# Folding the adaLN modulation into the query and key weights, with a reordered front part, in an attention and MLP kernel on one core

## The chip, the core and the metric

The kernel runs on one core of one Trainium2 chip. A core has a matrix engine (PE, with its weight loads listed apart as PEld), a vector engine (DVE), a scalar engine (ACT), a general engine (POOL) and a sequencer that issues most transfers (SP). Each engine takes its instructions in the order in which the program lists them, and engines wait for each other by semaphores. The metric is the device time of one execution in microseconds (us).

## The reference

One transformer block on 2048 rows of 512 numbers, with 32 heads of 16 and one key and value head for all (MQA). `c` gives six modulation vectors; only the first two (`sa`, `ca`) matter to the change.

```python
mod = (_silu(c) @ w_mod).reshape(c.shape[0], 6, 1, -1)
sa, ca, ga, sb, cb, gb = ...
h = _layernorm(x, axis=-1) * (1 + ca) + sa
q = h @ wq ; k = h @ wk ; v = h @ wv
o = softmax(q k^T * 16**-0.5) v @ wo
x = x + ga * o
h = _layernorm(x, axis=-1) * (1 + cb) + sb
x = x + gb * (gelu(h @ w1 + b1) @ w2 + b2)
```

## The kernel before

Products that must be exact run as three: each operand is split into a high part (rounded to the fast format fp32r) and the remainder, and `mm3` (L165) adds high x high, low x high and high x low. So a projection of 512 columns over four slices of 128 is 12 matrix instructions.

The program has a front part and a main loop. The main loop takes 64 units (a unit is 256 rows by 4 pairs of heads); per step it computes scores (`sexp`, L617), their exponentials on ACT (L621), the products with the values (`pv`, L638), and beside them the row maxima of a later unit: `Max.step` issues one score product (L512) that DVE reduces (L517). The maxima run ahead of the loop, which starts when 56 of them are done. A unit has 32; the 48th of the front is the last one of unit 0. When a unit has its 32, `put_max` turns them (L565, L566), POOL splits them in high and low (L560, L133, L140), and four small transfers (L555) put them as rows 48 and 49 into the unit's query tile `qst`. For unit 0 two of the four are issued by ACT. The first score product of the main loop (`e`) waits for these four.

The front part, for four blocks of 512 rows: load x (L229), mean and variance on DVE (`stats1`, L206 to L212), a power on POOL (L214), normalise in place (`xhat1`: L373 on DVE or POOL, L371 on ACT), turn on PE (`turn1`, L380, into banks e0, e1, e2 in turn), modulate and split (`mod1`: ACT reads the turned bank with scale `ca1` and bias `sa` at L386, then L135, L133 and L140 split it into `hH` and `hL`), key and value products (`kv_products`), their copies out (`kv_out`, L401 and L402; `low_k` on DVE, L407; `repeat_k` on ACT, L411), the query projection of group g (`qproj`) with its weights split by `prep_wq` (L342, L343). Queries go to memory (`send_q`, L424) and come back in another layout by six transfers a unit (`load_q`, L483).

The modulation vectors come first: `mod_rows` (L297) multiplies with `w_mod`, `mod_cols` (L301) turns the result into columns.

All five instruction streams are recorded in program order. After block 0 that order is written out by hand: `SLOTS` is a list of steps, a number meaning so many maxima and a name one step of the named job (`heads b` is `turn1` and the split of one slice, `keys b` one slice of the key products, `wq g` a `prep_wq`, `rows` a slice of the remaining modulation vectors). `keep_warm` issues products whose results nobody reads (L292).

## Time and profile before

| | us |
|---|---|
| median of 3 runs | 1556.17 (1555.15 to 1556.21) |
| the profiled execution | 1555.99 |
| its span, first to last instruction | 1554.1 |
| PE busy | 1537.9 (99% of the span) |
| DVE busy | 1398.3 (90%) |
| ACT busy | 1230.4 (79%) |
| POOL busy | 683.7 (44%) |
| first reduction of a maximum starts | 33.17 |
| last maximum of unit 0 reduced | 69.53 |
| first score product of the main loop starts | 75.14 |

Times in views are us from the span's start. A row of the timeline or of the groups reads: line of the kernel, engine, operation, what it writes and what it reads, shapes, count; in brackets the idle time before and what ended it. Busy spans of PE overlap, since products are pipelined, so the step from one product to the next is read from their starts.

### The profile page before, as it was taken

What the parts mean: (1) busy time and instruction counts of PE and PEld (TensorE: products, weight loads), DVE (VectorE), ACT (ScalarE), POOL (GpSimd) and SP (SyncE); (2) the same over time, 40 slices, a digit from 0 to 9 for tenths busy, and PEclk for the clock granted to TensorE, in tenths of its full rate; (3) what the DMA queues carried; (4) which work ended last, traced back from release to release, by engine and by line L of the source; (5) the groups of instructions that cost most, each with busy time, mean ns of one, the idle gap of its engine ahead of it and who ended that gap; (6) DMA issues with size and microseconds to landing.
All of it is one profiled execution on the core that took longest, in us unless ns stands there. A gap on an engine that the chain in (4) does not pass through costs nothing.

```text
span 1554.1 us, 41556 instructions
## 1 busy us (share of the span) xinstructions
PE 1537.9 (99%) x16405; PEld 954.4 (61%) x16405; DVE 1398.3 (90%) x2488; ACT 1230.4 (79%) x2401; POOL 683.7 (44%) x1206
## 2 busy tenths in 40 slices
PE   7999999999999999999999999999999999999999
PEld 4455555567655665557655676556655676566658
DVE  7999999999999999999999999999999999999814
ACT  5577778788877887788877888788877888778874
POOL 5535432867422571246521563235711574046511
PEclk9999999999999999999999999999999999999999
DMA  7226412413030220303112120302212230203141
GB/s 240 102 89 199 151 57 81 130 51 97 18 105 26 72 68 28 103 19 109 33 51 79 56 87 16 111 26 88 68 30 73 60 101 25 87 28 99 48 150 48
DMA packets 84215, 120.85 MB, mean 78 GB/s; under 512 B 21342, under 2 KB 57438, under 8 KB 83764
## 3 DMA queue, kind: packets, MB, share of 16 engines
q1 hardware_dynamic: 84004, 118.18, 23.7%
q8 instruction: 130, 2.13, 0.6%
q14 instruction: 65, 0.53, 0.1%
q10 hardware_dynamic: 16, 0.00, 0.0%
HBM read 90.87 MB, written 26.74 MB: 76 GB/s over the span
## 4 chain that ended last, share of the span: by engine, by line
PE 86%; DVE 8%; issue 3%; POOL 2%; DMA 1%; ACT 0%; SPq 0%; POOLq 0%; DVEq 0%
PE acc L638 29%; PE m L512 23%; PE e L617 16%; PE w1ps L198 8%; DVE mx L517 6%; PE w2ps L198 2%; PE w2ps L188 2%; DMA xt<-in_A_x_dram 1%; PE w1ps L188 1%; PE wops L198 1%; PE tp L198 1%; PE qps L198 1%; PE kps L165 1%; DVE st L823 0%; DVE x L816 0%
## 5 line engine op out<-in xcount | busy, mean ns | idle before, releaser
L517 DVE TENSOR_REDUCE mx<-m 128x1 f32<-128x512 f32 x2048 | 1270.6, 682 | 86.6 <-PE m L512 65.1
L621 ACT ACTIVATE p<-e 128x512 f32<-128x512 f32 x2048 | 1098.8, 598 | 255.1 <-PE e L617 112.0
L512 PE MATMUL m<-ks,qst 64*128 64x512 f32 x2048 | 836.7, 429 | 2.0 <-DVE mx L517 0.6
L617 PE MATMUL e<-qst,ks 64*128 64x512 f32 x2048 | 740.2, 412 | 0.0
L638 PE MATMUL acc<-p,va 128*32 128x256 f32 x8192 | 548.0, 385 | 0.0
L512 PEld LDWEIGHTS m<-ks,qst 64*128 64x128 f32 x2048 | 368.2, 184 | 205.1 <-DVE mx L517 173.5
L617 PEld LDWEIGHTS e<-qst,ks 64*128 64x128 f32 x2048 | 359.6, 184 | 89.3 <-ACT p L621 62.5
L638 PEld LDWEIGHTS acc<-p,va 128*32 128x32 f32 x8192 | 214.0, 109 | 213.9 <-issue 110.9
L198 PE MATMUL w1ps<-h2H,w1t 64*128 64x256 f32 x1232 | 235.5, 287 | 0.0
L560 POOL TENSOR_SCALAR mt<-turned 8x32 f32<-8x32 f32 x256 | 53.1, 208 | 399.9 <-DVE turned L566 387.9
L198 PEld LDWEIGHTS w1ps<-h2H,w1t 64*128 64x128 f32 x1232 | 186.0, 185 | 28.9 <-DVE mx L517 14.8
L198 PE MATMUL w1ps<-h2L,w1t 64*128 64x256 f32 x616 | 169.3, 275 | 0.0
L198 PE MATMUL w2ps<-w2H,gH 64*128 64x512 f32 x274 | 120.3, 439 | 0.0
L198 PEld LDWEIGHTS w1ps<-h2L,w1t 64*128 64x128 f32 x616 | 114.1, 185 | 0.0
L198 PE MATMUL w2ps<-w2L,gH 64*128 64x512 f32 x274 | 107.5, 392 | 0.0
L198 PE MATMUL w2ps<-w2H,gL 64*128 64x512 f32 x274 | 106.9, 390 | 0.0
L975 POOL TENSOR_SCALAR tt<-tt 128x256 f32<-128x256 f32 x77 | 31.0, 402 | 131.5 <-ACT tt L974 96.5
L140 POOL TENSOR_TENSOR gL<-z,gH 128x256 fp32r<-128x256 f32 x77 | 57.0, 741 | 6.4
L976 POOL TENSOR_TENSOR tt<-tt,z 128x256 f32<-128x256 f32 x77 | 56.7, 736 | 6.4
L986 POOL TENSOR_TENSOR z<-tt,z 128x256 f32<-128x256 f32 x77 | 56.4, 732 | 6.0
L985 POOL TENSOR_TENSOR tt<-tt,z 128x256 f32<-128x256 f32 x77 | 56.5, 733 | 0.0
L198 PEld LDWEIGHTS w2ps<-w2H,gH 64*128 64x128 f32 x274 | 50.4, 184 | 6.7 <-DVE ot L1038 2.5
(193 smaller groups left out, 1503.5 us busy)
## 6 DMA issues: line engine op xcount, KB each, us to landing
w1t<-dw SPq DMA_DIRECT2D x82, 512.0 KB
qst<-dq SPq DMA_DIRECT2D x384, 32.0 KB
do<-oc SPq DMA_DIRECT2D x62, 128.0 KB
dw<-w1s SPq DMA_DIRECT2D x11, 512.0 KB
xt<-in_A_x_dram SPq DMA_DIRECT2D x4, 1024.0 KB
dq<-qH SPq DMA_DIRECT2D x16, 256.0 KB
dq<-qL SPq DMA_DIRECT2D x16, 256.0 KB
x<-in_A_x_dram SPq DMA_DIRECT2D x8, 512.0 KB
```

What stands on the lines that cost most here:

```text
L140: eng_l.tensor_tensor(out=dst_l, in0=src, in1=raw(dst_h), op=ALU.subtract)
L188: nc.tensor.matmul(ps, a, b_, start=first_, stop=last_)
L198: ins = nc.tensor.matmul(ps, a[rows], b_[rows], start=first_ and s == 0, stop=last_ and s == 1)
L512: nc.tensor.matmul(m, qsts[u][rows, j, t * P:(t + 1) * P], ks[rows, kc * 512:(kc + 1) * 512], start=True, stop=True)
L517: nc.vector.tensor_reduce(out=self.mx[u][:, i, kc:kc + 1], in_=m, axis=AX.X, op=ALU.max)
L560: nc.gpsimd.tensor_scalar(out=mt[:, g:g + 32], in0=turned[g:g + 4 * T, :], scalar1=1.0, scalar2=0.0, op0=ALU.mult, op1=ALU.add)
L617: nc.tensor.matmul(e, ks[rows, kt * P:(kt + 1) * P], rhs, start=True, stop=True)
L621: ins = nc.scalar.activation(dst, e, AF.Exp, scale=0.25)
L638: ins = nc.tensor.matmul(accs[u][32 * cidx:32 * cidx + 32, :], va[:, kt, :], rhs, start=kt == 0, stop=kt == NKT - 1)
L976: nc.gpsimd.tensor_tensor(out=tt, in0=tt, in1=z, op=ALU.mult)
L985: nc.gpsimd.tensor_tensor(out=tt, in0=tt, in1=z, op=ALU.mult)
L986: nc.gpsimd.tensor_tensor(out=z, in0=tt, in1=z, op=ALU.add)
```

## The change

The modulation is no longer applied to the rows. With xn the normalised rows, (xn * (1 + ca) + sa) @ w is xn @ ((1 + ca) * w) plus sa @ w. So the weights are scaled by `ca1` before they are split, and `sa @ w` is added as a bias where the result is read.

- The modulation vectors come as columns from the start: 16 products of one column (`mod_cols`) for `ca`, 16 for `sa`, in place of eight products of 512 columns, a copy and four turns. The two halves of `w_mod` are loaded apart, `ca` first.
- `turn1` of block 0 follows each normalised tile, with the four `sa` products of a slice behind each tile's four turns. `split1` of block 0 reads the turned bank directly (ACT high, DVE low); in the other blocks ACT copies it (L438), ACT rounds it (L140) and POOL subtracts. Before, some of these parts were on DVE.
- `prep_wq` scales on POOL (L349), then a bias product (`bias_q`, four products of one column), ACT takes the column (`take_col`, L377), PE permutes it (`order_q`, L381), ACT takes it again (L382), and then come the casts. All that is in program order.
- Keys and values are read once over all 128 rows with bias (L450), the value copy is apart (`keep_v`, L459).
- The first unit's queries are placed by four products with selection matrices (`place_q`, L534) and a copy on ACT (L536). The second unit's still go through memory.
- The front part has another order: maxima start ahead of the splits of block 1. Blocks 1 and 2 are normalised on ACT, block 3 half on ACT and half on POOL. From slot 18 on (`WIDE`) every second maximum uses one of the banks e0 to e2. There are 20 warming products ahead, and nine in place of five ahead of the main loop.

The main loop is the same, but that the late projections add `bq` (L518).

```diff
-WARM = (4, 16, 2, 5)
+WARM = (20, 4, 4, 9)
...
+    load_mod(1)
...
+    load_mod(0)
     load_x(1)
-    nc.sync.dma_start(out=wqf[:, :, P:2 * P], in_=wqr[:, :, P:2 * P])
     load_x(2)
-    nc.sync.dma_start(out=wqf[:, :, 2 * P:D], in_=wqr[:, :, 2 * P:D])
     load_x(3)
+    nc.sync.dma_start(out=wqf[:, :, P:D], in_=wqr[:, :, P:D])
...
+    def mod_cols(ps, i, k):
+
+        for d in range(KD):
+            nc.tensor.matmul(ps[:, d:d + 1], wms[k][:, i, d * P:(d + 1) * P], cs[:, k:k + 1], start=k + d == 0, stop=k + d == 2 * KD - 2)
...
+    def scaled(dst, w, eng=nc.gpsimd):
+        eng.tensor_tensor(out=dst, in0=w, in1=ca1.unsqueeze(2).to_broadcast([P, KD, P]), op=ALU.mult)
...
+    def bias_q(ps, g):
+        for k in range(KD):
+            nc.tensor.matmul(ps, wqf[:, k, g * P:(g + 1) * P], sa[:, k:k + 1], start=k == 0, stop=k == KD - 1)
+
+    def take_col(src, g):
+        col = pro.tile([P, 1], F32, name=f"bqn{g}", tag="bqn", bufs=2)
+        nc.scalar.copy(col, src)
+        return col
+
+    def order_q(col, ps, g):
+        nc.tensor.matmul(ps, order, col, start=True, stop=True)
+        nc.scalar.copy(bq[:, g:g + 1], ps)
+
+    def prep_wq(g):
+        scale_wq(g)
+        ps = psum.tile([P, 2], F32, name=f"bq{g}", **ebank())
+        bias_q(ps[:, 0:1], g)
+        order_q(take_col(ps[:, 0:1], g), ps[:, 1:2], g)
+        split_wq(g)
...
+    def split1(b, d):
+
         hH, hL = hts[b]
-        h32 = pro.tile([P, BQ], F32, name=f"h32_{b}_{d}", tag="h32", bufs=4)
-        nc.scalar.activation(h32, tps.pop((b, d)), AF.Identity, scale=ca1[:, d:d + 1], bias=sa[:, d:d + 1])
-        split(hH[:, d, :], hL[:, d, :], h32, eng_h, eng_l, between)
+        ps = tps.pop((b, d))
+        if b == 0:
+            split(hH[:, d, :], hL[:, d, :], ps, act, dve)
+        else:
+            x32 = pro.tile([P, BQ], F32, name=f"x32_{b}_{d}", tag="h32", bufs=4)
+            nc.scalar.copy(x32, ps)
+            split(hH[:, d, :], hL[:, d, :], x32, act, pool)
...
     def kv_out(b):
-        for r in range(2):
-            nc.scalar.copy(ks[64 * r:64 * r + 48, cols], ps[64 * r:64 * r + 48, :])
-        nc.scalar.copy(vt[32:64, :], ps[32:64, :])
+        nc.scalar.activation(ks[:, cols], kps[b], AF.Identity, scale=kkeep, bias=kbias)
...
+    def place_q():
+
+        ps = psum.tile([P, 2, HQ], F32, name="q0ps", tag="m", bufs=3)
+        for j in range(2):
+            for part in range(2):
+                nc.tensor.matmul(ps[:, j, :], picks[:, part, j], first_qs[part][:, 0:HQ], start=part == 0, stop=part == 1)
+        qsts[0] = qbufs[0]
+        nc.scalar.copy(qbufs[0], ps)
...
+    for t, _ in enumerate(xhat1(0, dve)):
+        for d in range(KD):
+            turn1(0, d, [t])
+        mod_cols(ps, 0, t)
...
+    run(xhat1(1, act))
+    load_mods(0)
+    load_mods(1)
+    keep_warm(WARM[1], tag="x", bufs=1)
+    chunk(4)
+    keep_warm(WARM[2], tag="x", bufs=1)
+    stats1(3)
     load_mods(2)
-    repeat_k(0)
     run(xhat1(2, act))
-    run(xhat1(3, pool))
-    keep_warm(WARM[1])
+    run(xhat1(3, act, 2))
```

Three places of the order follow, first as it stood before and then as it stands in the changed kernel. A name is the tile, then block and slice where they matter (`x_1_0` is block 1, slice 0); `xt_150`, `xt_152`, `xt_154` are blocks 1, 2 and 3, and `xt_148` is block 2 before.

ACT, from the repeated keys of block 0 (`repeat_k`) on, before:

```order
L411 CAST ks<-ks 16x512
L371 ACTIVATE xt_148<-xt_148,nm_355,rs 128x512 x4
L401 CAST ks<-kps_489 48x512 x2
L402 COPY vt_508<-kps_489 32x512
L386 ACTIVATE h_2_0_524<-tp_0_519,sa,ca_67 128x512
```

The same place now:

```order
L463 CAST ks<-ks 16x512
L418 ACTIVATE xt_150<-xt_150,nm_382,rs 128x512 x4
L418 ACTIVATE xt_152<-xt_152,nm_423,rs 128x512 x4
L418 ACTIVATE xt_154<-xt_154,nm_475,rs 128x512 x2
L438 COPY x_1_0_493<-tp_0_488 128x512
L140 CAST bigH<-x_1_0_493 128x512
```

Before, the splits of block 1 stood ahead of this place; now ACT normalises ten tiles, the last two of block 3, ahead of the first split of block 1. On POOL, likewise, the two tiles of block 3 (L420) stand ahead of block 1's first remainder.

PE, from the last key products of block 2 on, before (the maxima are those of its keys, the last rows a slice of block 3's keys):

```order
L512 MATMUL m_0_1_1_0_681<-ks,qst_158 128x512
L512 MATMUL m_0_1_1_1_684<-ks,qst_158 128x512
L419 MATMUL vps_689<-ident,vt_508 128x32 x4
L165 MATMUL kps_699<-bigH,wkH 128x512
L165 MATMUL kps_699<-bigH,wkL 128x512
```

Now, where `wq 1` stands ahead of the first slice of block 3's keys:

```order
L428 MATMUL tp_3_710<-ident,xt_154 128x128 x4
L577 MATMUL m_1_1_1_0_719<-ks,qst_158 128x512
L577 MATMUL m_1_1_1_1_722<-ks,qst_158 128x512
L373 MATMUL bq_727<-sa,wqf 128x1 x4
L381 MATMUL bq_727<-bqn_732,order 128x1
L170 MATMUL kps_740<-bigH,wkH 128x512
```

A product that reads what ACT copied (`bqn_732`) now stands between maxima 32 and 33; ACT makes that copy behind the split of `x_3_3`. The same happens with `bq_823` ahead of maximum 43.

ACT, at the end of the front part, before:

```order
L555 DMA qst_157<-mh_824 1x4x128
L555 DMA qst_157<-ml_825 1x4x128
L342 CAST wqH<-wqf 128x4x64 x2
L1364 COPY modl_sb<-modl 128x512
L621 ACTIVATE p_897<-e_0_0_1_898 128x512
```

Now:

```order
L620 DMA qst_157<-mh_869 1x4x128
L620 DMA qst_157<-ml_870 1x4x128
L377 COPY bqn_904<-bq_899 128x1
L382 COPY cols<-bq_899 128x1
L368 CAST wqH<-wqm_897 128x4x64 x2
```

And PE there, now (the two first maxima are the 49th and 50th):

```order
L577 MATMUL m_0_0_2_0_887<-ks,qst_158 128x512
L577 MATMUL m_0_0_2_1_890<-ks,qst_158 128x512
L307 MATMUL modl<-wml_478,csb 32x512 x4
L373 MATMUL bq_899<-sa,wqf 128x1 x4
L381 MATMUL bq_899<-bqn_904,order 128x1
L577 MATMUL m_0_1_2_0_912<-ks,qst_158 128x512
```

The copy `bqn_904` stands behind ACT's two transfers of unit 0's maxima, and PE's product that reads it stands ahead of the last six maxima.

198 lines of the change are left out of this document (111 added, 87 removed), and 9 rows, old and new, of the table SLOTS.

## The prediction

> **What bounds the kernel now.** I read the page first, then stretches of time, then the chain of waits over the first 100 us, then the timeline of DVE. The page:
>
> ```profile
> span 1554.1 us, 41556 instructions
> PE 1537.9 (99%) x16405; PEld 954.4 (61%) x16405; DVE 1398.3 (90%) x2488; ACT 1230.4 (79%) x2401; POOL 683.7 (44%) x1206
> PE   7999999999999999999999999999999999999999
> ```
>
> Stretches of the main loop (busy us of each engine):
>
> ```profile
> 80.00:120.00 40.00, 40.00 (x422) 23.87 (x424) 37.36 (x65) 30.66 (x57) 16.48 (x28) 1.00 0.37 111
> 120.00:200.00 80.00, 80.00 (x842) 47.71 (x844) 74.15 (x128) 62.17 (x117) 43.97 (x63) 1.00 0.50 165
> ```
>
> From 80 us on PE is never idle, and the change leaves what PE does there alone. So the main loop keeps its length, and the time moves by as much as its start does: the first `e`. The chain of waits leading there:
>
> ```profile
> 28.27 3.64 PE idle L292 x16
> 31.91 0.44 PE m L512
> ...
> 73.82 1.40 PE idle L292 x5
> 75.21 0.42 PE e L617 x2
> ```
>
> PE reaches the first maximum through products that nobody reads: it was waiting for queries and keys. DVE from there:
>
> ```profile
> 33.17 1.29 DVE L517 TENSOR_REDUCE mx<-m 128x1 f32<-128x512 f32 x2
> ...
> 39.45 3.68 DVE L517 TENSOR_REDUCE mx<-m 128x1 f32<-128x512 f32 x6
> 43.30 4.87 DVE L517 TENSOR_REDUCE mx<-m 128x1 f32<-128x512 f32 x8 [0.16 <-PE m L512]
> ...
> 54.76 5.21 DVE L517 TENSOR_REDUCE mx<-m 128x1 f32<-128x512 f32 x8
> ...
> 67.05 2.48 DVE L517 TENSOR_REDUCE mx<-m 128x1 f32<-128x512 f32 x4 [1.05 <-PE m L512]
> ...
> 69.92 5.14 DVE L517 TENSOR_REDUCE mx<-m 128x1 f32<-128x512 f32 x8
> ```
>
> Eight maxima take 5.2, 0.65 each, and there are hardly gaps: between 33.17 and 75.06 DVE bounds the front part. Five marks serve below: first reduction at 33.17; 16th done at 45.9 (12 by 43.13, four more); 32nd at 57.4; 48th, the last of unit 0, at 69.53; first `e` at 75.14. The last two are tied by unit 0's transfers:
>
> ```profile
> 70.08 1.02 POOL L560 TENSOR_SCALAR mt<-turned 8x32 f32<-8x32 f32 x4 [0.33 <-DVE turned L566]
> ...
> 71.51 1.35 ACTq L555 DMA_DIRECT2D qst<-mh  x1
> 72.96 0.59 ACTq L555 DMA_DIRECT2D qst<-ml  x1
> ```
>
> ACT has issued both 4.0 after the 48th (73.55), and `e` follows 5.6 after it.
>
> **Prices**, from the groups of the first 76 us:
>
> ```profile
> L140 POOL TENSOR_TENSOR bigL<-h,bigH 128x512 fp32r<-128x512 f32 x10 | 13.1, 1336 | 0.8 <-ACT bigH L135 0.6
> L386 ACT ACTIVATE h<-tp,sa,ca 128x512 f32<-128x512 f32 x16 | 12.2, 775 | 1.6 <-POOL bigL L140 1.0 <-DVE ca L311 0.5
> L380 PE MATMUL tp<-ident,xt 128*128 128x128 f32 x64 | 10.0, 284 | 1.9 <-ACT h L386 1.9
> L206 DVE BATCH_NORM_STATS2 st<-xt 128x6 f32<-128x512 f32 x16 | 10.0, 680 | 1.4 <-DMA xt<-in_A_x_dram 1.4
> L373 POOL TENSOR_SCALAR xt<-xt,mv,rs 128x512 f32<-128x512 f32 x4 | 8.3, 2075 | 0.0
> L371 ACT ACTIVATE xt<-xt,nm,rs 128x512 f32<-128x512 f32 x8 | 6.0, 806 | 1.7 <-POOL b1c L273 1.7
> L135 ACT CAST bigH<-h 128x512 fp32r<-128x512 f32 x9 | 5.6, 620 | 0.3
> L407 DVE TENSOR_TENSOR ks<-kps,ks 16x512 fp32r<-16x512 f32 x4 | 2.7, 684 | 1.0 <-ACT vt L402 0.7
> L411 ACT CAST ks<-ks 16x512 fp32r<-16x512 f32 x4 | 2.5, 616 | 1.5 <-DVE ks L407 1.5
> L402 ACT COPY vt<-kps 32x512 f32<-32x512 f32 x4 | 2.3, 576 | 0.0
> L450 ACT COPY q<-qps 128x512 f32<-128x512 f32 x1 | 0.6, 585 | 4.0 <-PE qps L165 4.0
> L301 PE MATMUL modc<-ident,modr_sb 64*128 64x64 f32 x4 | 0.5, 235 | 0.0
> L165 PEld LDWEIGHTS qps<-h0H,wqH 128*128 128x128 f32 x8 | 1.5, 188 | 1.4 <-issue 1.0 <-POOL h0H L133 0.4
> ```
>
> **The change part by part.**
>
> *To the turned block 0.* Its last steps before:
>
> ```profile
> 8.34 5.17 PE L297 MATMUL modr<-wm,csb 128*32 128x512 f32 x16 [8.34 <-DMA wm<-in_w_mod_dram]
> ...
> 11.21 1.91 DVE L373 TENSOR_SCALAR xt<-xt,mv,rs 128x512 f32<-128x512 f32 x4 [1.16 <-POOL rs L214]
> ...
> 16.11 0.66 PE L380 MATMUL tp<-ident,xt 128*128 128x128 f32 x4 [0.61 <-ACT h L386]
> ```
>
> What goes: eight modulation products, a copy and four turns, ACT's L386 on block 0. What comes: 32 one-column products, two instructions each. No row shows one. Their step lies between 0.07 (L301: four in 0.46, 0.235 of it the last one's length) and 0.19 (a 128x128 weight load alone). I take 0.09, nearer L301, since loads overlap: 0.7 for a group of eight. Statistics start about where they did, three small DVE operations later, so normalised tiles leave DVE every 0.48 from 11.95 on, 0.25 later. Then PE does four turns (0.66 with the last one's 0.28, so about 0.44 when work follows) and a group (0.7) four times over, less the last group, and block 0 stands turned at T = 12.0 + 4 x 0.44 + 3 x 0.7 + 0.2 = 16.1 (15.6 at 0.07, 18.4 at 0.19). Scaled weights come in time: ca1 about 11.4 (it needs half of the `w_mod` bytes whose products ended at 13.5 before), 1.3 on POOL and about 2 of splitting: ready by 15.
>
> The Trainium skill (TensorE: Matmul & The Clock Gate, section LDWEIGHTS (loading the stationary operand)) puts a load of 128 columns at 128/1.2 = 107 ns whatever its rows; an estimate by that page would be 0.86 a group, T 0.5 later and a time of 1568.9. No run here shows the 128-row case.
>
> *To the first maximum.* The residues on DVE wait for sa at T + 0.9 and take 0.64 each. PE's 12 query products (0.23 each) begin at T + 0.6, with 17 bias products between them, and end at T + 5.8; ACT's high part (0.65) and DVE's low part (0.7) of the queries at T + 7.2. Key products run meanwhile (0.7 a slice; ACT and POOL have split their weights by T + 4.9), then four placing products (0.5), the last key slice (0.7), the key copy with bias (0.78 by L386), its low part on DVE (0.7): T + 11.1 = 27.2. DVE still has two statistics of block 2 and their sums: 1.8. First reduction at 29.05, **4.1 earlier**: the transfers of unit 0's queries are gone from the way.
>
> *First to 16th.* After four maxima (31.65) DVE takes block 3's statistics (4 x 0.62 and 0.55), which stood ahead of the maxima before. That ends at 34.7. POOL's power and mean follow, at their own pace of 1.6:
>
> ```profile
> 33.22 1.01 POOL L214 TENSOR_TENSOR rs<-ve,mhalf 128x4 f32<-128x4 f32 x1 [1.12 <-DVE ve L212]
> 34.30 0.20 POOL L361 TENSOR_TENSOR nm<-mv,rs 128x4 f32<-128x4 f32 x1
> 34.59 0.19 POOL L362 TENSOR_SCALAR nm<-nm 128x4 f32<-128x4 f32 x1
> 34.76 8.26 POOL L373 TENSOR_SCALAR xt<-xt,mv,rs 128x512 f32<-128x512 f32 x4
> ```
>
> So normalising block 3 starts at 36.3: two tiles on ACT to 37.85, two on POOL (2.07 each) to 40.4. All splits of block 1 are queued behind them. ACT's first copy frees a bank at 38.4 and lets the fourth turn and maximum 9 go; POOL's remainders come at 41.7, 42.95, 44.2, 45.45 (1.24 apart), and each lets one key slice and two maxima go. The 16th is done at 46.4, **0.5 later** than before; 3.9 of DVE's time was idle.
>
> *16th to 32nd.* Block 1's keys are complete only at 45.85; now key copy 0.78, low part 0.7, split of `x_2_0` 1.2, repeat 0.62 stand in one line before maxima 17 and 18. From there ACT needs 1.2 for a slice and DVE 1.3 for two maxima; DVE bounds again, the 27th is done at 55.6, the 32nd at 59.8: **2.4 later**.
>
> *32nd to 48th.* Maximum 30's product needs the bank that the 27th frees; behind it are the last key slice of block 2 (0.7) and then, on ACT in a row: key copy 0.78, split of `x_3_2` 1.2, repeat 0.62, value copy 0.58, split of `x_3_3` 1.2, `take_col` 0.2. PE stands at `order_q` until 61.6; with a key slice ahead, maximum 33 is reduced from 62.95: 3.1 idle. Next, low keys of block 3 wait for their copy, and 39 for scaled weights: 1.8. Then `order_q` of group 2 stands behind the query split (qps done 71.3; 0.7 + 0.62 + 0.2), values (0.4) and the product: 43 from 74.05 after 42 ended at 71.2, 2.85 idle. Sixteen maxima are 10.4 and 7.8 idle: the 48th at 77.9, **8.4 later**.
>
> *48th to `e`.* ACT's `take_col` stands behind its two transfers: 4.0 + 0.2 after the 48th, `order_q` 0.2, product 0.5, and maximum 51 is reduced 5.0 after it (DVE was free at 1.7). Six maxima take 3.9. The nine warming products use the bank e2 of the 54th, free 7.6 after the 48th, and last 9 x 0.23 = 2.05. So `e` comes 9.65 after the 48th instead of 5.6: at 87.5.
>
> *Nothing elsewhere.* The bias additions of the late projections replace copies of the same size on the same engines. In the main loop DVE has 3 us of 40 free, as in the stretch quoted; without that cover a bias would cost what L463's copy does already.
>
> **The sum.** -4.1 + 4.6 + 1.9 + 6.0 + 4.0 = +12.4 at `e`. Span 1554.1 + 12.4 = 1566.5; the execution takes 1.9 beyond its span (1555.99 against 1554.1), so 1568.4. The profiled execution is 0.2 under the median of the runs, so I say **1568**. Bounds: T moves it by -0.5 to +2.3; idle stretches that I took for waits of 3.9, 1.8 and 7.8 carry perhaps a third either way.
>
> **Rivals.**
>
> *DVE never starves (faster).* With queries placed on chip DVE starts at 29.05, and if ACT keeps ahead, it needs 56 x 0.65 + 3.05 of statistics + 3 x 0.69 + 0.4 = 41.9: it ends at 70.9 instead of 75.06, and the time is 1552. For it: that is how the front ran before, from 54 on. Against it: the four places above where PE's or ACT's order waits for a later thing. It decides at 4.1 of idle DVE time between the first and the 56th reduction; below that the change gains. 0.12.
>
> *Half of the waits are covered.* If ACT reaches both columns of groups 1 and 2 early, their 6.0 shrinks to 1 and the price is 1562 to 1563. The extra banks speak for it; that they lie behind ACT's splits, against. 0.15.
>
> *The array cools down.* The modulation products begin slow. Four of them between 10 and 10.8, then four between 11.9 and 12.4:
>
> ```profile
> L297 PE MATMUL modr<-wm,csb 128*32 128x512 f32 x4 | 2.0, 1062 | 0.0
> ...
> L297 PE MATMUL modr<-wm,csb 128*32 128x512 f32 x4 | 1.0, 593 | 0.0
> ```
>
> though PEclk reads 1.00 all along. PE was idle until 8.3 and slow for 3. Waiting at `order_q` it would be idle about 3.5 and then over 4; slow products afterwards cost about 1 at maximum 33 and 2 with the modulation rows and nine warming products: 1571. The Trainium skill (TensorE: Matmul & The Clock Gate, Part 1: The HAM clock gate) has the clock halved after an idle window of about 3.4 us; the two rows agree with half, and the length of idleness is shown by no row. 0.2.
>
> *It doesn't do what it says.* Turns start without the modulation, but its products stand between them and block 0 is turned at 16.1, hardly before the 16.8 of now; if placing costs what the transfers did and nothing starves, the time stays at 1556. 0.05.
>
> **Numbers.** The forecast has 0.48, with its own range of 1563 to 1573. Cases on the slower side together have 0.83 (0.48, 0.2, 0.15), the same 0.05, faster 0.12; 0.2%, 3 us, is what a measurement of this kernel can tell. The range of 1558 to 1574 reaches below the half-covered case and above the cold one at a late T.
>
> **What would show it.** First reduction near 29, the first `e` near 87; DVE idle by about 4 before the 16th maximum with PE waiting for POOL's `bigL`; PE's L381 released by ACT's L377 after about 3 of idleness, three times; nine idle products directly before `e`. The forecast is wrong if DVE's reductions run without gaps from 29 on, or if the main loop's stretches differ from those quoted.

## The result, and the profile after

The changed kernel takes 1593.86 us (median of 4 runs, 1591.85 to 1595.28) against 1556.19 for the kernel before on the same chip: **2.4% slower**, ratio 1.0242, 95% interval 1.0224 to 1.0259. The forecast of 1568.0 had the sign and missed the size by 25.9; 1593.86 lies outside the range of 1558 to 1574.

The head of the page of the changed kernel, with two rows of tenths in 40 slices, DVE's busy share and the granted clock:

```profile
span 1593.5 us, 41812 instructions
PE 1573.8 (99%) x16531; PEld 988.4 (62%) x16531; DVE 1397.7 (88%) x2489; ACT 1230.5 (77%) x2409; POOL 682.1 (43%) x1211
DVE  5659999999999999999999999999999999999914
PEclk7679999999999999999999999999999999999999
```

DVE and ACT work as long as before (1397.7 and 1230.5, against 1398.3 and 1230.4). What is new is the row of the granted clock: three slices, some 120 us, at 0.6 to 0.7. The main loop is untouched: from the first `e` to the end 1480.4 us (113.10 to 1593.5), before 1479.0. All but 1.4 us of the loss stands ahead of it, where the first `e` comes 38.0 later:

| in the profiled executions, us | before | forecast | after |
|---|---|---|---|
| block 0 turned | 16.8 | 16.1 | 20.25 |
| first maximum reduced from | 33.17 | 29.05 | 39.04 |
| 16th maximum done | 45.78 | 46.4 | 58.96 |
| 32nd | 57.24 | 59.8 | 78.38 |
| 48th | 69.53 | 77.9 | 99.42 |
| first `e` | 75.14 | 87.5 | 113.10 |

Where the clock was low, by the windows view of the changed kernel: a stretch and its length, the busy time of PE, of its weight loads, DVE, ACT and POOL with the instructions begun, then the granted clock, DMA share and GB/s. The stretches end where the clock changed:

```profile
4.95:11.78 6.83, 6.60 (x61) 6.52 (x59) 3.52 (x11) 0.17 (x1) 1.44 (x7) 1.00 1.12 349
11.78:32.26 20.48, 20.48 (x82) 18.71 (x83) 8.64 (x17) 4.32 (x10) 4.06 (x5) 0.50 0.66 219
32.26:39.09 6.83, 4.57 (x21) 3.06 (x19) 5.75 (x19) 3.86 (x6) 1.42 (x3) 1.00 0.33 107
39.09:45.91 6.82, 6.12 (x19) 4.18 (x19) 6.12 (x15) 4.55 (x7) 2.61 (x6) 0.50 0.84 308
45.91:49.33 3.42, 1.59 (x9) 0.80 (x8) 1.72 (x3) 3.14 (x5) 3.42 (x3) 1.00 0.01 2
49.33:59.57 10.24, 9.28 (x23) 4.92 (x22) 5.16 (x8) 3.21 (x7) 5.83 (x5) 0.50 0.32 104
59.57:62.98 3.41, 2.32 (x15) 1.36 (x13) 1.98 (x3) 3.30 (x6) 1.27 (x1) 1.00 0.00 0
62.98:73.22 10.24, 10.24 (x34) 5.86 (x33) 5.30 (x9) 4.92 (x11) 5.01 (x4) 0.50 0.31 102
73.22:80.05 6.83, 4.53 (x28) 3.20 (x26) 4.61 (x7) 5.04 (x9) 2.54 (x2) 1.00 0.00 1
80.05:86.87 6.82, 6.76 (x20) 4.02 (x21) 2.35 (x4) 1.12 (x5) 3.71 (x4) 0.50 0.00 0
86.87:103.94 17.07, 13.69 (x82) 7.76 (x80) 9.90 (x18) 4.79 (x12) 6.36 (x12) 1.00 0.09 32
103.94:114.18 10.24, 9.29 (x30) 4.84 (x32) 3.77 (x6) 1.63 (x5) 1.66 (x3) 0.50 0.09 19
```

Six stretches at exactly half, 64.8 us together. The first begins at 11.78, while PE is busy 6.60 of the 6.83 before it. The last 3.42 of these, and then the timeline of PE, which shows with what it was busy:

```profile
8.36:11.78 3.42, 3.19 (x30) 3.11 (x29) 2.22 (x9) 0.17 (x1) 1.04 (x1) 1.00 1.18 297
```

```profile
7.87 3.68 PE L312 MATMUL modc<-cs,wm 128*128 128x1 f32 x32
11.78 1.11 PE L428 MATMUL tp<-ident,xt 128*128 128x128 f32 x4 [0.23 <-DVE xt L420]
12.69 1.71 PE L312 MATMUL modc<-cs,wm 128*128 128x1 f32 x8
14.25 1.10 PE L428 MATMUL tp<-ident,xt 128*128 128x128 f32 x4
```

So the fall did not follow a pause. Up to 7.87 the warming products ran; then thirty-two one-column instructions fill the time ahead of the fall, 0.115 each. Behind it eight of them take 1.71, 0.21 each, and a round of four turns and eight products 2.46 (11.78 to 14.25) where the forecast had 0.44 + 0.7.

The waits that the forecast named are all there. PE's timeline has a turn that waits for ACT's copy and a key product that waits for POOL's remainder (`bigL`), both ahead of the 16th maximum, then the ordering products behind ACT's column copy, and the idle products directly ahead of `e`; DVE's has the holes that follow:

```profile
48.32 0.66 PE L428 MATMUL tp<-ident,xt 128*128 128x128 f32 x4 [1.83 <-ACT x L438]
51.52 0.80 PE L170 MATMUL kps<-bigL,wkH 128*128 128x512 f32 x1 [0.96 <-POOL bigL L145]
...
80.11 0.59 PE L381 MATMUL bq<-bqn,order 128*128 128x1 f32 x2 [2.36 <-ACT bqn L377]
94.53 0.38 PE L381 MATMUL bq<-bqn,order 128*128 128x1 f32 x2 [0.70 <-ACT bqn L377]
103.79 0.48 PE L381 MATMUL bq<-bqn,order 128*128 128x1 f32 x2 [2.22 <-ACT bqn L377]
108.96 4.21 PE L297 MATMUL idle<-wkH 128*128 128x512 f32 x9 [0.95 <-DVE mx L582]
113.10 0.80 PE L682 MATMUL e<-qst,ks 64*128 64x512 f32 x2
```

```profile
49.44 1.29 DVE L582 TENSOR_REDUCE mx<-m 128x1 f32<-128x512 f32 x2 [1.63 <-PE m L577]
53.07 1.29 DVE L582 TENSOR_REDUCE mx<-m 128x1 f32<-128x512 f32 x2 [2.34 <-PE m L577]
55.37 1.29 DVE L582 TENSOR_REDUCE mx<-m 128x1 f32<-128x512 f32 x2 [1.01 <-PE m L577]
...
82.95 1.29 DVE L582 TENSOR_REDUCE mx<-m 128x1 f32<-128x512 f32 x2 [4.57 <-PE m L577]
...
95.74 3.68 DVE L582 TENSOR_REDUCE mx<-m 128x1 f32<-128x512 f32 x6 [3.31 <-PE m L577]
...
105.03 1.29 DVE L582 TENSOR_REDUCE mx<-m 128x1 f32<-128x512 f32 x2 [3.96 <-PE m L577]
```

DVE waits for PE's `m` each time. The nine idle products take 4.21 (0.47 each, at half clock) where the forecast had 2.05. Two readings fit: a slow PE, or an order full of waits. The runs part them.

### The profile page after: what moved, and what is told of

Read it like the earlier page. It is cut to its first block, busy times and chain, and to the rows that moved or that the text cites. A ratio compares the mean times of both kernels' runs of the same rounds, so it can differ in the third digit from the quotient of the medians.

```text
span 1593.5 us, 41812 instructions
## 1 busy us (share of the span) xinstructions
PE 1573.8 (99%) x16531; PEld 988.4 (62%) x16531; DVE 1397.7 (88%) x2489; ACT 1230.5 (77%) x2409; POOL 682.1 (43%) x1211
## 4 chain that ended last, share of the span: by engine, by line
PE 89%; DVE 8%; DMA 1%; POOL 1%; ACT 1%; SPq 0%; issue 0%; ACTq 0%; DVEq 0%; POOLq 0%
PE acc L703 30%; PE m L577 25%; PE e L682 16%; PE w1ps L203 8%; DVE mx L582 6%; PE w2ps L203 2%; PE w2ps L193 2%; PE w1ps L193 1%; PE kps L170 1%; PE qps L203 1%; PE wops L203 1%; PE tp L203 1%; PE qps L170 0%; PE tp L428 0%; DVE st L888 0%; DMA wml<-in_w_mod_dram 0%
```

## The experiments

The marks of each run's profiled execution, in us, as in the table above; "half" is the time at half clock from the first full stretch on, up to 120 us; the ratio is to the kernel before on the same chip, with its 95% interval.

| run | block 0 turned | first max | 16th | 32nd | 48th | first `e` | half | median | ratio |
|---|---|---|---|---|---|---|---|---|---|
| after | 20.25 | 39.04 | 58.96 | 78.38 | 99.42 | 113.10 | 64.8 | 1593.86 | 1.0242 (1.0224 to 1.0259) |
| e1_fill | 20.08 | 34.35 | 53.12 | 70.94 | 92.39 | 102.62 | 6.8 | 1585.12 | 1.0184 (1.0155 to 1.0214) |
| e2_rows_mod | 18.01 | 34.54 | 54.45 | 74.02 | 96.78 | 108.19 | 51.2 | 1590.77 | 1.0221 (1.0191 to 1.0250) |
| e3_bias_once | 19.43 | 37.63 | 61.54 | 77.05 | 93.47 | 103.27 | 51.2 | 1586.87 | 1.0196 (1.0166 to 1.0225) |
| e4_before_cold | 16.66 | 33.04 | 47.95 | 59.41 | 71.70 | 77.44 | 10.2 | 1559.39 | 1.0017 (1.0006 to 1.0029) |
| e5_fill_lean | 21.31 | 35.58 | 53.19 | 69.12 | 89.06 | 99.29 | 3.4 | 1581.58 | 1.0159 (1.0129 to 1.0188) |
| e6_fill_bias | 21.64 | 35.91 | 59.83 | 75.78 | 94.46 | 103.03 | 23.9 | 1586.97 | 1.0193 (1.0164 to 1.0223) |
| e7_stats_early | 20.16 | 39.04 | 58.96 | 74.25 | 95.35 | 106.81 | 47.8 | 1592.53 | 1.0229 (1.0189 to 1.0269) |
| e9_parts_fill | 15.47 | 33.33 | 50.97 | 66.88 | 86.81 | 97.03 | 10.2 | 1580.15 | 1.0153 (1.0133 to 1.0173) |
| e10_bias_early | 20.90 | 35.16 | 52.52 | 69.23 | 88.94 | 96.21 | 10.2 | 1579.50 | 1.0149 (1.0129 to 1.0169) |
| e12_no_columns | 15.45 | 29.30 | 49.23 | 64.75 | 84.26 | 97.01 | 27.3 | 1579.34 | 1.0143 (1.0123 to 1.0164) |
| e14_no_columns_fill | 16.93 | 30.80 | 48.16 | 64.10 | 84.24 | 94.49 | 6.8 | 1575.55 | 1.0124 (1.0103 to 1.0144) |
| e8_best1 | 14.68 | 30.15 | 48.10 | 62.69 | 75.79 | 82.21 | 10.2 | 1566.02 | 1.0055 (1.0032 to 1.0078) |
| e11_best2 | 14.92 | 28.71 | 43.17 | 60.32 | 73.38 | 79.18 | 10.2 | 1560.70 | 1.0028 (1.0018 to 1.0038) |
| e13_best3 | 14.91 | 32.92 | 48.37 | 69.61 | 82.67 | 88.49 | 20.5 | 1570.12 | 1.0084 (1.0067 to 1.0101) |
| e15_best4 | 14.70 | 26.51 | 39.95 | 58.82 | 73.37 | 79.28 | 6.8 | 1561.29 | 1.0033 (1.0021 to 1.0046) |
| e16_best5 | 14.89 | 26.69 | 40.98 | 59.57 | 73.42 | 79.24 | 6.8 | 1561.77 | 1.0036 (1.0022 to 1.0050) |

### Hold the clock, leave the order

```diff
+    def fill(n, at):
+        if at not in fills:
+            fills[at] = psum.tile([P, BQ], F32, name=f"fill_{at}", tag=at[0])
+        for _ in range(n):
+            nc.tensor.matmul(fills[at], picks[:, 0, 0], picks.rearrange("p a b c -> p (a b c)"), start=True, stop=True)
...
         mod_cols(ps, 1, k)
+        fill(3, "m")
...
         mod_cols(ps, 0, t)
+        fill(2, "m")
...
+        if i < 16:
+            fill(2, "x")
```

> The changed kernel with dense 512-column products of no use added on TensorE: three behind each of the four groups that make 1 + scale, two behind each group of a turned tile, three among the bias products, 20 instead of 8 around the first four maxima, two ahead of each of the first 16 slots, eight behind the bias products of groups 1 to 3; some 85 more products, 18 us of work at 0.215. Nothing else is moved. Theory A (the halved clock is the surplus over the forecast): the granted clock reads 1.00 through nearly all of the first 100 us, block 0 is turned about when it was (20 to 21, since the fillers cost there what the clock gives), and from there on the front runs near the forecast's pace: first e at 90 to 96 instead of 113, time 1571 to 1577. Theory B (the waits in the order of ACT, POOL and PE are the loss, and the clock is low only because PE waits): fillers add work and shorten no wait, e at 112 to 120, time 1593 to 1601.

Work was added and 8.7 us went: 6.8 us at half instead of 64.8, `e` 10.5 earlier. Theory B, which had more work and no gain, falls. But theory A had `e` at 90 to 96 and 1571 to 1577, and missed both. A part of that are fillers in slots that had no room for them. Without these, with `fill(8, "x")` ahead of the first maximum and `if i in (0, 1, 2, 3, 8, 9, 10, 15)`:

> The first experiment (dense products of no use in the changed kernel) with 20 of the 85 fillers left out: none in the eight slots whose key products follow one another without a wait (4 to 7 and 11 to 14), four fewer ahead of the first maximum. In that experiment the clock read 1.00 except for 6.8 us, the first e came at 102.62 instead of 113.10, and two fillers a slot (0.43) stood between maxima that DVE then waited 0.5 for. Theory A (clock first, waits second): without them the 16th to 32nd maximum take 13.5 to 15.5 instead of 17.8, first e at 98 to 101, time 1579 to 1583, so that the clock is worth 12 to 15 of the 25 that the forecast missed. Theory B (the gap before each pair is a wait for ACT or POOL): the stage stays at 17 to 18, time 1584 to 1587. If the key products alone don't hold the clock it falls again, and the time goes back to 1588 or more.

1581.58 and `e` at 99.29, as theory A had it; the 16th to 32nd maximum take 15.93 instead of 17.8, a little more than its 13.5 to 15.5. With the clock full but for 3.4 us, `e` is 13.8 earlier than in the changed kernel and still 11.8 later than forecast.

### What lets the clock fall

In `e2_rows_mod` the modulation's one-column products give way to streamed rows, a copy and turns:

```diff
-    for k in range(KD):
-        mod_cols(ps, 1, k)
+    for k in range(KD):
+        mod_rows(ps, k, [wms[k][:, 1, :]])
...
-        mod_cols(ps, 0, t)
+        mod_rows(ps, t, [wms[t][:, 0, :]])
+    ps = mod_turned(ps, 0, tag="m", bufs=3)
```

> The changed kernel with the modulation made as before it: the vector spread to 32 columns as weights, the modulation matrix streamed 512 columns wide (four products of about 0.85 each for either half), a copy and four turns for either half. No one-column product stands before block 0 is turned; TensorE's time there is about the same. Theory A, with the one-column products as what first lets the clock fall: granted clock 1.00 up to about 27, block 0 turned at 16 to 18 instead of 20.1, first reduction at 29 to 32 instead of 39.0; the later falls (waits for xhat and order_q) stay, time 1575 to 1586. Rival C (one-column products are only longer than priced, the clock falls for other reasons): clock halved from about 12 on as now, block 0 turned at 19 to 21, time 1590 to 1597.

The clock no longer falls at 11.78. It falls behind the next one-column products, those of the biases, and again not after a pause: PE is busy 3.30 of the 3.42 us ahead of the fall (19.95 to 23.37). PE's timeline, then two windows of the same run:

```profile
21.33 0.95 PE L379 MATMUL biases<-sa,wqf 128*128 128x1 f32 x8
22.14 1.03 PE L1395 MATMUL biases<-sa,wk 128*128 128x1 f32 x8
```

```profile
6.30:23.37 17.07, 16.15 (x82) 8.43 (x82) 8.52 (x22) 4.13 (x11) 4.06 (x5) 1.00 1.01 331
23.37:26.78 3.41, 3.41 (x11) 2.73 (x10) 1.48 (x4) 0.68 (x3) 1.28 (x1) 0.50 0.74 186
```

So block 0 was turned at 18.0, as theory A had it, but the first maximum came at 34.54, not by 32, and the time of 1590.77 is rival C's number. `e9_parts_fill` makes each half of the modulation as four pieces of 128 columns side by side in the array, keeps the lean fillers elsewhere, and still has the biases' one-column products:

```diff
+        for d in range(KD):
+            nc.tensor.matmul(ps[32 * d:32 * d + 32, :], csb[:, k, :], wms[k][:, i, d * P:(d + 1) * P], start=k == 0, stop=k == KD - 1)
...
+        nc.scalar.copy(rows, ps)
+        psc = psum.tile([P, KD, 32], F32, name=f"{name}_c", **place)
+        nc.tensor.transpose(psc.rearrange("p d c -> p (d c)"), rows, ident)
```

> The lean fillers of the fifth run, with the one-column products of the modulation replaced: each half is made as four row pieces of 128 columns side by side (16 products, about 1.1 for a half), one copy and one turn. So fillers no longer stand between the turns of block 0. In the fifth run the clock was full but for 3.4 us and the front was still 5.2 late when block 0 was turned (21.3 against the forecast's 16.1). Theory: that lateness is the one-column products and the fillers that they made necessary, and nothing else: block 0 turned at 14 to 15.5, first maximum at 28.5 to 31 instead of 35.6, first e at 92 to 95 instead of 99.3, time 1573 to 1577. Rival: what follows waits for something that comes at its own time (a load, statistics of block 1), then the first maximum moves by less than half of that, and e is at 96.5 or later.

Block 0 was turned 5.8 earlier than in `e5_fill_lean`, the first maximum came only 2.3 earlier: the rival's number, for another reason than it gave. The clock fell at 18.85 for 6.8 us. That fall can't be put down to the bias products alone: they begin only at 17.83, and PE stands idle for 0.6 of the 3.42 us ahead of the fall. The next run goes back to the changed kernel without fillers and replaces all one-column products:

```diff
+        nc.tensor.matmul(ps[0:32, :], sab[:, k, :], wqf[:, k, 0:P], start=k == 0, stop=k == KD - 1)
+        nc.tensor.matmul(ps[32:64, :], sab[:, k, :], wk0[:, k, :], start=k == 0, stop=k == KD - 1)
...
-        bias_q(ps[:, 0:1], g)
-        order_q(take_col(ps[:, 0:1], g), ps[:, 1:2], g)
+            nc.tensor.matmul(ps[0:32, :], sab[:, k, :], wqf[:, k, g * P:(g + 1) * P], start=k == 0, stop=k == KD - 1)
...
+        nc.tensor.transpose(psc, rows[0:32], ident[0:32, 0:32])
```

> The changed kernel without fillers and in its own order, with every one-column product made as row pieces: the modulation's halves (four pieces of 128 columns side by side), the biases of group 0 and of the keys (two pieces side by side), those of groups 1 to 3 (one piece in each slot that had the ordering product; the ordering is done by the copy, and a turn takes the ordering product's place, so its wait for ACT stays). Theory A, with one-column products as what begins the falls: block 0 turned at 14.5 to 16 (forecast 16.1), clock full until the first maxima, first maximum at 28 to 31 (forecast 29.05), and so the forecast's front comes out up to there; behind it the clock falls in the waits that the forecast had (16th, 33rd, 43rd, 51st maximum), first e at 95 to 103, time 1575 to 1583. If the clock falls before 25 with no one-column product in the program, sparse work of any kind does it, not these products: first maximum at 32 or later.

Windows of this run, then the row of its first maximum:

```profile
7.60:31.49 23.89, 19.04 (x154) 12.55 (x154) 19.61 (x49) 11.40 (x23) 7.94 (x12) 1.00 0.84 271
31.49:34.90 3.41, 3.41 (x15) 2.51 (x13) 3.38 (x11) 2.41 (x4) 0.10 (x1) 0.50 0.91 320
34.90:38.32 3.42, 0.88 (x4) 0.37 (x2) 2.13 (x4) 1.90 (x3) 3.25 (x4) 1.00 0.71 287
38.32:51.97 13.65, 13.12 (x33) 7.14 (x33) 5.90 (x10) 6.39 (x12) 7.34 (x7) 0.50 0.23 78
...
89.52:96.34 6.82, 5.87 (x19) 2.91 (x17) 3.75 (x6) 0.34 (x2) 1.66 (x3) 0.50 0.11 24
```

```profile
29.30 2.48 DVE L596 TENSOR_REDUCE mx<-m 128x1 f32<-128x512 f32 x4
```

Theory A's numbers all hold in this run. Without a one-column product, without a filler and in the changed kernel's own order, the clock is full from 7.6 to 31.5, and the first maximum is reduced at 29.30. The forecast said 29.05. PE was busy less there (19.04 of 23.89, 80%) than ahead of the first fall in the changed kernel (6.60 of 6.83, 97%). Behind it the clock falls in waits: 27.3 us.

### What the order costs with the clock held

`e12_no_columns` with the lean fillers from the first maximum on:

```diff
-    keep_warm(WARM[1], tag="x", bufs=1)
+    fill(8, "x")
...
+        if i in (0, 1, 2, 3, 8, 9, 10, 15):
+            fill(2, "x")
```

> The twelfth run's kernel (no one-column product, the changed kernel's order) with the lean fillers of the fifth from the first maximum on: eight ahead of the first maximum and eight behind the fourth instead of four each, two ahead of the slots 0 to 3, 8 to 10 and 15, eight behind the bias products of groups 1 to 3. This is the front as the forecast had it: full clock, no long one-column products, every wait in its place. If the forecast's terms were right and only the clock and the columns were missing, the marks come out as it said: first reduction 29 to 30 (29.05), 16th maximum 45 to 48 (46.4), 32nd 60 to 63 (59.8), 48th 78 to 82 (77.9), first e 88 to 92 (87.5), time 1568.5 to 1573. If e stays at 95 or more, the waits themselves were priced too low, by the difference.

Its windows from mark to mark, first to 16th maximum and on to `e`:

```profile
30.80:48.16 17.36, 14.92 (x63) 9.51 (x64) 13.03 (x25) 11.01 (x18) 11.88 (x12) 0.90 0.53 185
48.16:64.10 15.94, 14.80 (x77) 9.04 (x75) 11.80 (x19) 11.54 (x21) 8.37 (x7) 1.00 0.21 66
64.10:84.24 20.14, 19.47 (x104) 11.17 (x105) 10.68 (x18) 7.58 (x19) 8.03 (x10) 1.00 0.07 27
84.24:94.49 10.25, 7.84 (x45) 4.59 (x41) 5.34 (x10) 1.06 (x4) 4.24 (x10) 1.00 0.07 20
```

The forecast's terms make 17.35, 13.4, 18.1 and 9.6 for these. The first is exact, the others are 2.5, 2.0 and 0.6 short, 5.2 in all with rounding. So the 95 of the other case was nearly reached, and 1575.55 is above the 1573 expected. `e` is 7.0 later than forecast: 1.75 before the first maximum, the rest in these three terms. They are upper bounds for the waits, since fillers stand between the maxima, too. And the first term is exact by luck: the clock was at half from 32.4 to 35.8 (0.90 in the row), ten fillers took 4.14 there, and PE waited for `bigL` once, for 0.97, not four times as forecast.

Up to the first maximum this is the program of `e12_no_columns`, but here the clock fell, from 11.9 to 15.3, with no one-column product in it. That is the sign that the expectation of `e12_no_columns` had set against theory A. The window ahead of this fall, and one of `e12_no_columns` that kept the clock:

```profile
8.49:11.90 3.41, 1.69 (x29) 0.61 (x25) 2.21 (x9) 0.44 (x2) 1.04 (x1) 1.00 1.17 301
...
24.66:28.08 3.42, 1.94 (x8) 1.02 (x6) 2.94 (x9) 2.49 (x4) 1.42 (x3) 1.00 0.21 64
```

PE is busy half of the first, since its products wait for pieces of `w_mod`. The next window of `e12_no_columns` is as busy as the one shown, 1.94 of 3.41, and lost the clock at 31.49. So one-column products are one way to lose the clock and thin work is another; with PE about half busy it went either way.

The queries' biases moved elsewhere, in two ways. All at once between the fourth maximum and block 1's turns, alone and with the lean fillers:

```diff
-        bias_q(ps[:, 0:1], g)
-        order_q(take_col(ps[:, 0:1], g), ps[:, 1:2], g)
+        for g in range(1, KD):
+            bias_q(ps[:, 0, g - 1:g], g)
...
+        if i == 1:
+            order_rest(*rest_q)
```

> The changed kernel with the query biases of groups 1 to 3 made together between the first four maxima and block 1's turns (24 one-column instructions, one copy, one ordering product, one copy), so that no ordering product stands in the slots. Theory B (waits in order): the three stalls of 2.36, 0.70 and 2.22 at the ordering product and the 4.6 and 4 of idle DVE behind them go: e 7 to 10 earlier, time 1584 to 1587. Theory A: the same stalls go and with them two of the six falls of the clock (at 80.0 and 103.9, 17 us at half): e 10 to 16 earlier, time 1578 to 1584; up to 70 us the clock reads as now or worse.

> The lean fillers and the query biases of groups 1 to 3 made at once, together; nothing else. Clock and order waits, if these are two separate costs, add up: the stalls at three ordering products (2.4, 0.7, 2.2 in the changed kernel, with idle DVE of 4.6, 3.3 and 4.0 behind them) go as well, first e at 88 to 94, time 1569 to 1575. That would be the forecast's mechanisms without the clock and with two thirds of its order waits gone, and so still above the kernel before. If the two are one cost counted twice: 1578 or more.

Alone it took 7.0 off, with `e` 9.8 earlier, both as theory B had them. With fillers it lost what the fillers had gained, 1586.97 against 1581.58, and the expectation of 1569 to 1575 was wrong by far. The edit had made a wait, and it also left out the 24 fillers that had stood behind the bias products; the clock was at half again from 83.1 to 96.7. PE's and DVE's timelines of `e6_fill_bias`:

```profile
48.87 1.22 PE L310 MATMUL fill_x<-picks 128*128 128x512 f32 x2 [4.95 <-ACT cols L406]
```

```profile
50.85 1.29 DVE L599 TENSOR_REDUCE mx<-m 128x1 f32<-128x512 f32 x2 [9.59 <-PE m L594]
```

The next fillers write the bank of the biases and wait for ACT's copy out of it, which stands behind normalised tiles and the first splits of block 1; clock at half from 42.1 to 52.4. So this run doesn't tell whether clock and waits add. Then with the bias products and column copies of groups 1 to 3 a few slots ahead (`"bq 1"` three slots before `"wq 1"`, and so on) and no fillers between:

> The lean fillers of the fifth run, with the bias products and the column copies of groups 1 to 3 two or three slots ahead of the ordering products, and without the 24 fillers that stood between the two. The forecast's mechanism (the ordering product waits for a copy that is queued on ACT behind splits and transfers, 3.1 and 2.85 idle on DVE for groups 1 and 2 and part of 5.0 for group 3): if it is the cause of these gaps, the idle of 5 before the 33rd and of 4 before the 43rd maximum shrink to under 2, first e at 92 to 96 instead of 99.3, time 1574 to 1578. If the gaps are really waits for splits of block 3 or for keys, they stay and so does the time, 1580 to 1583.

`e` at 96.21, 3.1 earlier, just outside the expected 92 to 96, and 1579.50 is above the expected 1574 to 1578. DVE's idle before the 33rd maximum is 0.26 instead of 3.99, before the 43rd 2.02 instead of 4.48, before the 51st 0.45 instead of 3.57. The mechanism was right. But 4.9 of idle came in before the 39th, 46th and 47th (PE waits 2.09 for a column copy ahead of the 46th), and the clock was at half from 81.5 to 88.4, perhaps for want of the 24 fillers.

`e7_stats_early` moves block 1's statistics and normalising ahead (`stats1(1)` before the copy of `sa`, `run(xhat1(1, act))` behind the first queries):

> The changed kernel with the statistics of block 1 moved on DVE ahead of the shift's copy (DVE is idle there for 5.7) and its normalising on ACT ahead of the placed queries; nothing for the clock. Theory of the order (block 1's chain of statistics, POOL's power, ACT, turns starts 13 us later than before the change, and everything behind it waits): normalised tiles of blocks 2 and 3 are 3 to 5 earlier, first maximum at 37 to 38.5, 16th maximum at 54 to 56 instead of 59.0, time 1588 to 1591. Theory A: PE at half clock sets the stretch from 40 to 75 whatever is ready, the 16th maximum moves by 1.5 at most and the time stays within 1591 to 1596.

First and 16th maximum did not move at all, which theory A had and the theory of the order had not: what was ready earlier met a PE at half clock up to 32.1. Later stages were shorter, and the two runs, 1589.94 and 1595.12, lie apart.

### The kernel before without its warming products

`WARM = (0, 0, 0, 0)` in the kernel before:

> The kernel before with its 27 warming products left out, nothing else. Theory A: what keeps its clock up in the front is gone, the granted clock reads 0.50 in several stretches of the first 75 us and the time rises by 8 to 25, to 1564 to 1581. Theory B: DVE sets that front, PE has room, and the time stays within 1553 to 1558.

Two of its windows:

```profile
31.80:38.62 6.82, 6.52 (x14) 4.21 (x15) 3.75 (x11) 3.18 (x5) 5.37 (x5) 0.50 0.52 155
38.62:79.58 40.96, 38.34 (x179) 19.00 (x177) 36.34 (x60) 22.70 (x43) 22.89 (x28) 1.00 0.26 98
```

The clock falls there, too, in one stretch ahead of `e` (and in a short one behind it), but the price is 2.6 us, a ratio of 1.0017; both theories missed. In that stretch DVE waits (3.75 of 6.82 busy); from then on the clock stays, DVE sets the pace (36.34 of 40.96), and from the 16th maximum to the 48th the marks lie as far apart as with the products. The warming products are worth little here, and a single fall is no disaster where the order leaves PE room.

### Can the idea be made to pay?

Five kernels that keep the folded weights and placed queries, with no one-column product in the modulation and the order mended after the trace of the run before: pieces instead of columns, `sa` after block 0's turns, block 1's statistics early, fewer idle products ahead of `e`.

```diff
     for t, _ in enumerate(xhat1(0, dve)):
         for d in range(KD):
             turn1(0, d, [t])
-        mod_cols(ps, 0, t)
...
+    for k in range(KD):
+        row_parts(ps, k, csb, wms[k][:, 0, :])
...
-WARM = (20, 4, 4, 9)
+WARM = (18, 0, 0, 4)
```

> A version made from what the first runs showed: the folded weights and the placed queries stay, but the modulation halves and the biases of groups 1 to 3 are made as four row pieces of 128 columns side by side in the array (32 equal weight columns each) and one turn, so that one-column products are left only for group 0 and the keys; the shift is made after block 0 is turned; block 1's statistics and normalising come before the maxima, block 3's normalising after block 1's turns; a few dense fillers; four idle products, in another bank, ahead of e; the last maxima in their own banks. If clock and order together are the whole loss: block 0 turned at 13.5 to 15, first maximum at 23 to 27, first e at 70 to 80, time 1549 to 1560. If the placed queries and folded weights carry a cost of their own that none of this touches: 1565 or more.

> The eighth run's kernel mended where its trace showed waits: in that run TensorE stood 0.7 to 1 at the bias of group 0 and fell to half clock from 22.1 to 25.5, DVE was idle from 18.8 to 23.5 for it, and the statistics of blocks 1 and 2 came only behind it. Here the shift is made right behind block 0's turns, the biases of group 0 and the keys are row pieces too (no one-column product is left), the statistics of block 1 stand on DVE before the queries and those of block 2 before the first maximum, the biases of groups 1 to 3 later, in a slot; the last weight scaling no longer stands ahead of the first shift's gathering on POOL. First maximum at 24 to 27 instead of 30.2, 16th at 41 to 44, first e at 73 to 78 instead of 82.2, time 1552 to 1558. If the key blocks' splits on ACT set the pace instead of DVE's maxima, e stays at 80 or later and the time at 1562 or more.

`e8_best1` came out at 1566.02, the number of its rival; its clock fell at 22.1, behind one-column biases and a pause of 0.66. `e11_best2`, without them and with statistics and biases in other places, came out at 1560.70: it gives back 33 of the 38 us, but misses its 1552 to 1558. The next moved the statistics of block 1 on DVE and the normalising of blocks 2 and 3:

> The eleventh run's kernel with three waits of its trace taken out: the statistics of block 1 no longer stand behind the copies of the biases on DVE, those of block 2 come whole before the low keys of block 0; normalising of block 2 stands behind block 1's splits on ACT, that of block 3 behind block 2's first ones; the biases of groups 1 to 3 are spread over three slots, so that TensorE doesn't stand 1.2 for ACT's copy (2.85 of idle DVE at the 19th maximum). First maximum at 26 to 28, 16th at 40 to 42, 32nd at 52 to 56 instead of 60.3, first e at 72 to 76 instead of 79.2, time 1553 to 1557: level with the kernel before or a little faster. If ACT's splits set the pace from the 16th on, e stays at 77 or later and the time at 1558 or more.

It went the wrong way, to 1570.12. PE's timeline:

```profile
24.39 0.80 PE L173 MATMUL kps<-h0H,wkL 128*128 128x512 f32 x1 [3.55 <-POOL wkL L148]
```

POOL's power of the moved statistics now stood ahead of the key weights' remainder in its queue. With that and block 3's normalising mended:

> The thirteenth run's kernel with its two new waits mended: the low part of the key weights stands ahead of block 1's power on POOL again (TensorE waited 3.55 for it), and block 3's normalising comes two slots earlier (turns of block 3 waited 1.1 and 1.7 for it). First maximum at 25.5 to 28 instead of 32.9, 16th at 40 to 43, first e at 74 to 78, time 1554 to 1559, so level with the kernel before or a little above it; at 1553 or less the folded weights and placed queries would pay.

The first maximum comes at 26.51, 6.7 before the kernel before, and the 16th at 39.95, 5.8 before it. Then it is lost again: `e` at 79.28 and 1561.29, not the 74 to 78 and 1554 to 1559 expected. Windows of the first to 16th and the 16th to 32nd maximum:

```profile
26.51:39.95 13.44, 13.19 (x60) 7.84 (x61) 13.00 (x25) 12.26 (x20) 7.70 (x9) 1.00 0.66 246
39.95:58.82 18.87, 16.02 (x99) 9.71 (x96) 11.80 (x20) 12.67 (x25) 13.81 (x12) 0.91 0.18 59
```

DVE is busy 13.00 of 13.44, then 11.80 of 18.87, and one window at half clock lies in the second (42.7 to 46.1). The last run reordered that stretch (block 3 normalised on ACT alone, block 2's turns two slots earlier):

> The fifteenth run's kernel with one stretch reordered: in that run the front was 5.8 ahead of the kernel before at the 16th maximum (39.95 against 45.78) and gave it all back between the 16th and the 32nd (18.9 against 11.5), DVE idle 7.1 there, with POOL in block 3's normalising (4.1) ahead of block 2's remainders and ACT in turns that came late. Here block 3 is normalised on ACT alone, block 2's turns and splits begin two slots earlier, its key products lie among the maxima of block 1's keys, block 3's turns before those of its keys. If that order is the loss: 16th to 32nd in 12 to 14.5, first e at 73 to 77, time 1553 to 1557, level with the kernel before or a little faster. If ACT has no room for it (its work from the 4th to the 56th maximum is some 30 of 50): e at 78 or later, 1559 or more, and the folded weights and placed queries pay nothing here.

`e` at 79.24, as without it: that order was not the loss. The numbers are those of the case that ACT has no room, but ACT is busy only 12.67 of the 18.87 in the row above. Whether another order would do better, or what else holds the stretch, wasn't settled. None of these kernels beats the kernel before; the nearest is 0.28% slower (interval 0.18 to 0.38%).

## Why the prediction was wrong, step by step

**The step that failed** is the clock. The sum went by full speed throughout: "I take 0.09, nearer L301, since loads overlap" for the one-column products, and the rival that the array cools down was given 3 us, "about 1 at maximum 33 and 2 with the modulation rows and nine warming products". That mechanism stood there with a chance of 0.2, but it was looked for only in PE's pauses late in the front. It came at 11.78, out of the change's own products, and returned in the waits; in place of 3 it was worth about 20 (below).

The 25.6 us by which `e` is later than forecast divide so:

- 0.25 up to the first maximum, where `e12_no_columns` has 29.30 and the forecast 29.05. That it is so little is in part luck: T is 15.45 there instead of 16.1, with other products, and the chain behind it takes 13.85 instead of 11.1 + 1.8.
- 9.7 up to the first maximum (39.04 against that 29.30): the one-column products at their half-clock price and all that followed at half clock. T itself: three rounds of 2.46 instead of 1.14 make 4.0, and T is 4.15 later than forecast. At full clock 0.115 an instruction lies within the bounds of 0.07 to 0.19 and would have cost 0.025 more for each of the 24 instructions that T counts, so 0.6.
- 10.4 from the first maximum to `e` (74.06 against 63.69 in `e14_no_columns_fill`): half clock in the waits. In `e12_no_columns`, without fillers, this stretch takes 67.71.
- 5.2 in that stretch with the clock held, 63.69 against the forecast's 58.45: waits priced too low, above all between the 16th and the 32nd maximum, where the forecast had DVE as the bound from the 17th on and DVE stood idle for 4.1 of 15.94, in gaps of 0.2 to 0.8. Some of it is the fillers' own: eight stand in that stretch, and behind the 32nd they ran 0.7 and 1.5 past ACT's copies that they were to cover.

That division takes two kernels for two halves and assumes that they add; up to the first maximum the two are one program, and their executions differ by 1.5 there.

Point by point:

- *First to 16th, POOL's `bigL` behind block 3's normalising*: the wait is there, 0.96 once in the changed kernel and 0.97 in `e14_no_columns_fill`. That 17.36 meets 17.35 is luck, since the other idle time of DVE there has other causes (a filler stretch at half clock, ACT's copies).
- *Ordering products behind ACT's copies, three times*: right in place; in size 2.36, 0.70 and 2.22 of PE's time, where about 3 was forecast, and 4.57, 3.31 and 3.96 idle on DVE against 3.1, 2.85 and 5.0, at half clock in part. With the copies early the first gap shrank from 3.99 to 0.26.
- *Nine idle products directly ahead of `e`*: right, 4.21 long at half clock instead of 2.05.
- *Nothing elsewhere, the main loop as it was*: right, 1480.4 against 1479.0.
- *DVE never starves*, *half of the waits are covered*, *doesn't do what it says*: none; DVE was busy 40.85 of 63.69 us in the best execution of this order.
- *The array cools down*: right in kind, but it was put at 3 and was about 20 (9.7 and 10.4). The Trainium skill (TensorE: Matmul & The Clock Gate, Part 1: The HAM clock gate) has free-running windows of 3413 ns, and the trace agrees: each stretch above is 3.41, 6.83, 10.24, 17.07 or 20.48, multiples of 3.41. It calls for an idle window ahead of a fall; the trace differs, with PE busy 3.19 of the 3.42 us ahead of the first fall, and the trace decides.
- The same page's section LDWEIGHTS (loading the stationary operand) gives 128/1.2, so 107 ns, for a load of 128 columns. The 0.115 of the row of 32 is near it at full clock; at half clock the row says 0.21.
- *The sign and the chances*: slower at 0.83 was right; the range stopped at 1574 because its cold case charged half clock with 3 us and left the front ahead of it at full speed.
- *Slips that nothing hangs on*: the kernel before has its 16th and 32nd maximum done at 45.78 and 57.24, not 45.9 and 57.4, and T at 0.19 an instruction sums to 18.5, not 18.4.

## What to carry to other kernels

When a change puts many tiny products on PE, or takes dense work out of a stretch, first ask what it does to the clock there: price that stretch at half speed as a case of its own, down to the end of the stretch, not only its pauses. Make vectors of weights by streaming the matrix past a few equal columns and turning the result once, not by one column per load: in `e12_no_columns` sixteen such products took 1.28 us where sixteen one-column products had taken 3.68, and the clock held. Leave room in such a stretch all the same: in `e14_no_columns_fill` it fell there for one window. And when a job is moved past a queue, list every later job of all engines in that queue: two of the edits here took a wait out and put a longer one in (`e6_fill_bias` with ACT's copy of the biases, `e13_best3` with POOL's power).
